# Two head masks moved from GpSimd to VectorE at the start of a convolution-and-MLP kernel

## Chip, cores, metric

One core of a Trainium2 chip. The metric is the device time of one execution in microseconds. A profile's span is some 1.8 us shorter than the time of the same run. All positions below are microseconds from the start of the profile's span.

## The reference

```python
# x [8, 4096, 192], weight [8 heads, 7 taps], w_in [192, 2048], w_out [2048, 192]
w = softmax(weight, axis=-1)
x_pad = concatenate([zeros((B, 6, D)), x], axis=1)       # causal, 7 taps
a = einsum('hk,bskhg->bshg', w, x_unf)                   # one filter per head of 24 channels
h = a.reshape(32768, 192) @ w_in
g = where(h > 0, h, exp(minimum(h, 0)) - 1)
out = g @ w_out
```

## The kernel before

The kernel works through 32 tiles of 1024 tokens. For each, TensorE convolves with a banded weight matrix `Tm`, multiplies by `w_in` into PSUM (`H`), ScalarE takes the exponential into `E`, GpSimd clips it, VectorE combines it with `H` into `gT`, and TensorE multiplies by `w_out`. The kernel gives each engine its own list of instructions and joins the lists by semaphores. The first tile goes another way, so that TensorE starts early: x is loaded as it is (`xs`), cast (`xb`), transposed on TensorE (`xT`) and convolved with diagonal weights (`taps`). The diagonal needs each partition's own head weights. They come from one small matmul with a head mask `owner`, and the band comes from another with the weights spread by a block mask `block8`. GpSimd makes both masks before it issues any DMA:

```python
# GpSimd
g.memset(ones[:], 1.0).then_inc(s_id)
W(s_id, 1)
g.affine_select(out=ident[:], in_=ones[:], ...).then_inc(s_id)
for step in range(2):                                  # owner: two selects
    W(s_id, 2 + step)
    g.affine_select(out=owner[:, :], in_=owner[:, :] if step else ones[0:HEADS, :], ...).then_inc(s_id)
W(s_id, 4)
g.affine_select(out=block8[:, :, :], ...).then_inc(s_id)
load_w_in(0); load_w_in(1); load_w_out(0)              # 7 DMA issues
for gr in range(2): load_x(1, gr)                      # 2
load_w_out(1); load_w_out(2)                           # 2
for gr in range(2): load_x(2, gr)                      # 2
for i, (n, u) in enumerate(units):
    for to_load in x_before.get(i, ()): load_x(*to_load)   # one more at i = 0
    W(s_exp, i + 1)
    g.tensor_scalar(out=E[:, i % NE, :], ..., op0=ALU.min, op1=ALU.max).then_inc(s_clp)

# VectorE
v.memset(zw[:], 0.0); v.memset(wband[:], 0.0); v.memset(xbh[...], 0.0)
W(s_wb, 1); W(s_wq, 16)
v.tensor_reduce(wmx[:], wq[:], AXIS.X, ALU.max)        # softmax of the weights begins
# ... [cut]
W(s_id, 5); W(s_set, 5)
v.tensor_tensor(wnb[:], block8[:], wn[:, :].unsqueeze(1).to_broadcast(...), ALU.mult)

# TensorE, matmul with owner
W(s_id, 4); W(s_set, 6)
```

Of the kernel before, what the change touches and what calls it, by code (L numbers as in the profile page):

```python
# [5 lines left out]
ALU = mybir.AluOpType  # L6
# [7 lines left out]
HP = 64  # L14
FC = 128
D = 192
HEADS = 8
KSIZE = 7
# [53 lines left out]
def bass_lightweight_conv__then__act_elu_kernel(  # L72
# [46 lines left out]
    gt_at, turned, att_at, conv_begun, step = {}, {}, {0: 0.0}, {}, [0]  # L119
# [226 lines left out]
    for second in range(2):  # L346
        for rt in range(2):
            g = rt ^ second
            k, b = divmod(NP - O_AT[g], NB)
# [64 lines left out]
    with ExitStack() as stack:  # L414
        def sbuf(name, shape, dt):
            return stack.enter_context(nc.sbuf_tensor(name, shape, dt))
# [4 lines left out]
        def sema(name):  # L421
            return stack.enter_context(nc.semaphore(name))
# [3 lines left out]
        ident = sbuf("ident", [P, P], BF16)  # L426
        ones = sbuf("ones", [P, P], BF16)
# [25 lines left out]
        owner = sbuf("owner", [HEADS, P], BF16)  # L453
        block8 = sbuf("block8", [HEADS, HEADS, KSIZE], BF16)
# [11 lines left out]
        s_scr = sema("s_scr")  # L466
        s_x = [[sema(f"s_x{i}_{g}") for g in range(2)] for i in range(NXB)]
        s_id = sema("s_id")
        s_xs = sema("s_xs")
        s_xh = sema("s_xh")  # L470
        s_wb = sema("s_wb")
# [143 lines left out]
        @block.gpsimd  # L615
        def _gpsimd(g: bass.BassGpSimd):
            W = Waits(g)

            def load_x(s, gr):
                b = s % NXB  # L620
                if s >= NXB:
                    W(s_cv, CU * (s - NXB))
                if s == NXB:
                    W(s_zw, 1)
                def windows(w0, w1, rows):
                    src = bass.AP(
                        tensor=x_flat.tensor,
                        offset=(s * SUP + gr * GS + w0 * CW - PAD) * D,
                        ap=[[D, rows], [CW * D, w1 - w0], [1, D]],
                    )  # L630
                    g.dma_start(  # L631
                        xg[0:rows, b, 2 * w0 + gr : 2 * w1 : 2, :], src
                    ).then_inc(s_x[b][gr], 16)

                if s == NS - 1 and gr == 1:
                    windows(0, NWIN - 1, P)
                elif gr == 2:
                    W(s_xl, 16)
                    g.tensor_copy(xg[0:XL, b, 2 * NWIN - 1, :], xl[:, :]).then_inc(s_xc)
                else:  # L640
                    windows(0, NWIN, P)

            def batch_zeros(s):

                W(s_x[s % NXB][0], x_need[s, 0])
                g.memset(xg[0:PAD, s % NXB, 0, :], 0.0).then_inc(s_z)

            def load_w_in(k):
                c0, c1 = WCOLS[k]
                for j in range(3):  # L650
                    g.dma_start(  # L651
                        w_in[0:HP, j, c0:c1],
                        bass.AP(
                            tensor=moe_w_in.tensor,
                            offset=8 * j * FF + c0,
                            ap=[[CPH * FF, HEADS], [FF, 8], [1, c1 - c0]],
                        ),
                    ).then_inc(s_w[k], 16)

            def load_w_out(k):  # L660
                q = slice(WOUT[k], WOUT[k + 1])
                g.dma_start(  # L662
                    w_out[:, q, :], moe_w_out.rearrange("(q p) d -> p q d", p=FC)[:, q, :]
                ).then_inc(s_w[3 + k], 16)

            g.memset(ones[:], 1.0).then_inc(s_id)  # L666
            W(s_id, 1)
            g.affine_select(  # L668
                out=ident[:],
                in_=ones[:],  # L670
                pattern=[[-1, P]],
                compare_op=ALU.is_equal,
                fill=0.0,
                base=0,
                channel_multiplier=1,
            ).then_inc(s_id)
            for step in range(2):
                W(s_id, 2 + step)
                g.affine_select(  # L679
                    out=owner[:, :],  # L680
                    in_=owner[:, :] if step else ones[0:HEADS, :],
                    pattern=[[0, 2], [1 - 2 * step, HP]],
                    compare_op=ALU.is_ge,
                    fill=0.0,
                    base=7 * step,
                    channel_multiplier=8 * (2 * step - 1),
                ).then_inc(s_id)
            W(s_id, 4)
            g.affine_select(  # L689
                out=block8[:, :, :],  # L690
                in_=ones[0:HEADS, 0 : HEADS * KSIZE].rearrange("p (h k) -> p h k", h=HEADS),
                pattern=[[1, HEADS], [0, KSIZE]],
                compare_op=ALU.is_equal,
                fill=0.0,
                base=0,
                channel_multiplier=-1,
            ).then_inc(s_id)
            load_w_in(0)
            load_w_in(1)
            load_w_out(0)  # L700
            for gr in range(2):
                load_x(1, gr)
            load_w_out(1)
            load_w_out(2)
            for gr in range(2):
                load_x(2, gr)
            for i, (n, u) in enumerate(units):
                s, at_n = divmod(i // 2, NQ)
                if i % 2 == 0 and at_n == ZERO_AT and (s + 2) % SPB == 0 and s + 2 < NS:
                    batch_zeros(s + 2)  # L710
                for to_load in x_before.get(i, ()):
                    load_x(*to_load)
                W(s_exp, i + 1)
                g.tensor_scalar(  # L714
                    out=E[:, i % NE, :],
                    in0=E[:, i % NE, :],
                    scalar1=1.0,
                    scalar2=0.0,
                    op0=ALU.min,
                    op1=ALU.max,  # L720
                ).then_inc(s_clp)
# [50 lines left out]
        def _vector(v):  # L772
            W = Waits(v)

            v.memset(zw[:], 0.0).then_inc(s_zw)  # L775
            v.memset(wband[:], 0.0).then_inc(s_wb)
            v.memset(xbh[:, :, :, :], 0.0).then_inc(s_xz)
            W(s_wb, 1)
            W(s_wq, 16)
            v.tensor_reduce(wmx[:], wq[:], AXIS.X, ALU.max).then_inc(s_set)  # L780
# [2 lines left out]
                out=wq2[:],  # L783
# [11 lines left out]
                out=wn[:],  # L795
# [2 lines left out]
                scalar2=None,  # L798
                op0=ALU.mult,
            ).then_inc(s_set)  # L800
            W(s_id, 5)
            W(s_set, 5)
            v.tensor_tensor(
                wnb[:],
# [32 lines left out]
            for i in range(ON_DVE):  # L837
# [3 lines left out]
                if i == 0:  # L841
                    ins = v.tensor_scalar(
                        out=part[:], in0=src, scalar1=w, scalar2=None, op0=ALU.mult
                    )
                else:
                    W(s_part, i)
                    ins = v.scalar_tensor_tensor(
                        out=part[:], in0=src, scalar=w, in1=part[:], op0=ALU.mult, op1=ALU.add
# [11 lines left out]
            for item in dve_order:  # L860
# [6 lines left out]
                if s >= NG3:  # L867
# [4 lines left out]
                    out=gT[:, s % NG3, q, u, :],  # L872
# [8 lines left out]
        def _tensor(pe):  # L881
            W = Waits(pe)
# [18 lines left out]
            for item in pe_order:  # L901
# [6 lines left out]
                    for _ in range(item[2]):  # L908
                        pe.matmul(H[:, bank, :], zw[:, 0:P], zw[:, 0:GS], start=True, stop=True)  # L909
                elif item[0] == "s":  # L910
                    W(s_id, 4)
                    W(s_set, 6)
                    pe.matmul(
                        H[:, bank_of["d", 2], 0:KSIZE],
# [73 lines left out]
                elif item[0] == "c":  # L988
# [13 lines left out]
                    h = HU * u + q  # L1002
# [36 lines left out]
                else:  # L1039
                    _, k, g, rt, q, kb, visit, ends = item  # L1040
# [93 lines left out]
```

## Time and profile before

| | before |
|---|---|
| median of the 3 runs given first | 718.48 us (718.13 to 719.18) |
| profile span | 716.6 us |
| TensorE busy | 710.7 us |
| x (`xs`) lands | 5.41 |
| first hidden-layer matmul | 10.55 |
| first clip on GpSimd | 12.86 |
| `Tm` lands, first convolution matmul | 18.70, 19.14 |

A line of a timeline gives the start, the length, the engine, the source line, the operation with what it writes and reads, how often it ran in a row, and in brackets the idle time before it with what ended it. Two lines of GpSimd's timeline of the kernel before:

```profile
2.43 3.56 POOL L651 DMA_DIRECT2D w_in<-in_moe_w_in_dram  x6
...
12.86 8.10 POOL L714 TENSOR_SCALAR E<-E 128x512 f32<-128x512 f32 x14
```

There is no bracket at the first clip: GpSimd came to it straight from a DMA issue, so it was GpSimd that was late. The intent of the change follows from this.

### The profile page before, as it was taken

How to read it: one execution, taken by the hardware profiler on the slowest of the kernel's cores; microseconds unless marked ns; L12 is line 12 of the kernel's file. 1: busy time of each engine (PE TensorE's matmuls, PEld its weight loads, DVE VectorE, ACT ScalarE, POOL GpSimd, SP SyncE). 2: the span in 40 equal slices, each digit the busy share in tenths (PEclk: the TensorE clock that was granted, in tenths of full speed). 3: DMA queues.
4: the chain of work that ended last, by engine and by line, in shares of the span. 5: the costliest groups of instructions: out<-in, count | busy, mean ns of one | idle time of the engine just before them, and what ended most of it. 6: DMA issues, size and time to landing. Idle time of an engine off the chain costs nothing.

```text
span 716.6 us, 27662 instructions
## 1 busy us (share of the span) xinstructions
PE 710.7 (99%) x11873; PEld 681.6 (95%) x11873; DVE 641.5 (90%) x1049; ACT 677.4 (95%) x1290; POOL 663.6 (93%) x1112
## 2 busy tenths in 40 slices
PE   8999999999999999999999999999999999999998
PEld 4699999999999999999999999999999999999998
DVE  7999889998898998899998999988989988999994
ACT  6999999999999999999999999999999999999994
POOL 9999999999999999999999999999999999999893
PEclk9999999999999999999999999999999999999999
DMA  9635334564433544444554344544445534444212
GB/s 183 99 72 95 65 73 78 93 86 76 80 79 74 95 89 64 80 85 79 87 91 69 73 76 95 87 73 76 85 73 91 93 63 78 87 80 83 63 43 69
DMA packets 132303, 58.80 MB, mean 82 GB/s; under 512 B 98374, under 2 KB 131412, under 8 KB 132180
## 3 DMA queue, kind: packets, MB, share of 16 engines
q0 software_dynamic: 43504, 16.77, 22.4%
q1 hardware_dynamic: 88388, 39.37, 22.0%
q8 instruction: 93, 1.52, 0.9%
q10 hardware_dynamic: 288, 0.88, 0.4%
q14 instruction: 30, 0.25, 0.1%
HBM read 34.63 MB, written 25.46 MB: 84 GB/s over the span
## 4 chain that ended last, share of the span: by engine, by line
PE 96%; POOL 2%; ACT 1%; DVE 0%; issue 0%; DVEq 0%; POOLq 0%
PE H L1052 54%; PE H L1029 37%; PE H L1004 4%; POOL xg L631 1%; ACT E L760 1%; POOL E L714 1%; POOL w_in L651 0%; POOL w_out L662 0%; DVE gT L871 0%; ACT csb L756 0%; POOL owner L679 0%; DVE osb L862 0%; POOL block L689 0%; POOL ident L668 0%; POOL ones L666 0%
## 5 line engine op out<-in xcount | busy, mean ns | idle before, releaser
L871 DVE SCALAR_TENSOR_TENSOR gT<-E,H 128x512 f16<-128x512 f32 x1024 | 631.8, 681 | 62.8 <-POOL E L714 58.4
L1029 PE MATMUL H<-att,w_in 64*128 64x512 bf16 x3072 | 679.8, 376 | 1.2 <-DVE gT L871 0.9
L1052 PE MATMUL H<-w_out,gT 64*128 64x192 f16 x8192 | 680.4, 243 | 0.1
L714 POOL TENSOR_SCALAR E<-E 128x512 f32<-128x512 f32 x1024 | 603.0, 611 | 41.1 <-ACT E L760 34.2
L1052 PEld LDWEIGHTS H<-w_out,gT 64*128 64x128 f16 x8192 | 606.7, 94 | 17.5 <-PE H L1052 1.5
L760 ACT ACTIVATE E<-H 128x512 f32<-128x512 f32 x1024 | 585.0, 601 | 23.9 <-PE H L1029 0.4
L1029 PEld LDWEIGHTS H<-att,w_in 64*128 64x128 bf16 x3072 | 275.3, 93 | 7.8 <-DVE gT L871 2.9
L1004 PE MATMUL H<-xg,Tm 64*128 64x240 bf16 x496 | 90.9, 263 | 0.0
L756 ACT ACTIVATE csb<-H 112x480 bf16<-112x480 f32 x124 | 70.7, 570 | 0.4 <-PE H L1004 0.3
L767 ACT ACTIVATE osb<-H 128x384 f32<-128x384 f32 (+1 forms) x129 | 62.0, 482 | 6.9 <-PE H L1052 6.8
L631 POOL DMA_DIRECT2D xg<-in_x_dram x62 | 54.7, 884 | 0.2 <-issue 0.2
L1004 PEld LDWEIGHTS H<-xg,Tm 64*128 64x128 bf16 x496 | 42.6, 94 | 1.2 <-DVE gT L871 0.3
L862 DVE COPY osb<-H 128x192 f32<-128x192 f32 x1 | 0.4, 357 | 7.3 <-PE H L1052 7.3
L909 PE MATMUL H<-zw 128*128 128x512 bf16 x10 | 4.3, 588 | 1.2 <-DVE zw L775 1.2
L909 PEld LDWEIGHTS H<-zw 128*128 128x128 bf16 x10 | 1.2, 134 | 3.0 <-issue 1.7
L651 POOL DMA_DIRECT2D w_in<-in_moe_w_in_dram x6 | 3.6, 612 | 0.0
L736 ACT ACTIVATE xb<-xs 128x512 bf16<-128x512 f32 x2 | 1.2, 622 | 2.4 <-DMA xs<-in_x_dram 2.4
L978 PE MATMUL H<-xT,taps 64*64 64x256 bf16 (+1 forms) x50 | 2.6, 317 | 0.0
L662 POOL DMA_DIRECT2D w_out<-in_moe_w_out_dram x3 | 2.5, 853 | 0.0
L978 PEld LDWEIGHTS H<-xT,taps 64*64 64x64 bf16 x50 | 2.0, 106 | 0.5 <-issue 0.2
L729 ACT ACT_TABLE_LOAD x1 | 1.3, 1283 | 1.2 <-PEq L1119 1.2
L936 PEld LDWEIGHTS H<-ident,xb 64*64 64x64 bf16 x48 | 1.2, 126 | 0.8 <-ACT xb L736 0.8
(45 smaller groups left out, 20.5 us busy)
## 6 DMA issues: line engine op xcount, KB each, us to landing
out_dram<-osb SPq DMA_DIRECT2D x126, 192.0 KB, 2.9
xg<-in_x_dram POOLq DMA_DIRECT2D x61, 240.0 KB, 4.5
xs<-in_x_dram ACTq DMA_DIRECT2D x1, 768.0 KB, 4.6
w_in<-in_moe_w_in_dram POOLq DMA_DIRECT2D x6, 128.0 KB, 4.7
att<-csb SPq DMA_TRANSPOSE x31, 3.9
w_out<-in_moe_w_out_dram POOLq DMA_DIRECT2D x2, 192.0 KB, 7.9
w_out<-in_moe_w_out_dram POOLq DMA_DIRECT2D x1, 384.0 KB, 11.8
w_in<-w_in SPq DMA_DIRECT2D x1, 336.0 KB, 6.8
```

What stands on the lines that cost most here:

```text
L631: g.dma_start(xg[0:rows, b, 2 * w0 + gr : 2 * w1 : 2, :], src).then_inc(s_x[b][gr], 16)
L651: g.dma_start(w_in[0:HP, j, c0:c1], bass.AP(tensor=moe_w_in.tensor, offset=8 * j * FF + c0, ap=[[CPH * FF, HEADS], [FF, 8], [1, c1 - c0]], ...
L714: g.tensor_scalar(out=E[:, i % NE, :], in0=E[:, i % NE, :], scalar1=1.0, scalar2=0.0, op0=ALU.min, op1=ALU.max,).then_inc(s_clp)
L756: a.activation(*conv_evac(W, m), ACT.Copy).then_inc(s_ce)
L760: a.activation(E[:, i % NE, :], H[:, bank_of[item], :], ACT.Exp).then_inc(s_exp)
L767: a.activation(*out_evac(W, *item[1:]), ACT.Copy).then_inc(s_oev[item[2]])
L871: v.scalar_tensor_tensor(out=gT[:, s % NG3, q, u, :], in0=E[:, i % NE, :], scalar=1.0, in1=H[:, bank_of[item], :], op0=ALU.subtract, op1=A ...
L909: pe.matmul(H[:, bank, :], zw[:, 0:P], zw[:, 0:GS], start=True, stop=True)
L978: ins = pe.matmul(H[to, bank_of["d", j] + (j == 2 and c0 > 0), c0:c1], taps[rows, tap, rows], xT[rows, j, HALO - PAD + tap + c0 : HALO - P ...
L1004: ins = pe.matmul(H[:, bank_of["c", m], 256 * q : 256 * q + UC], Tm[rows, h, :], xg[rows, s % NXB, :, CPH * h : CPH * (h + 1)].rearrange(" ...
L1029: ins = pe.matmul(H[:, bank_of[item[:3]], :], w_in[HP * r : HP * (r + 1), j, FC * q : FC * (q + 1)], att[HP * r : HP * (r + 1), s % 2, j, ...
L1052: ins = pe.matmul(acc_of(k, g)[:, D * kb : D * (kb + 1)], gT[HP * rt : HP * (rt + 1), t % NG3, q, g, t0 : t0 + P], w_out[HP * rt : HP * (r ...
```

## The change

The masks are copies of parts of the identity, so VectorE, which waits for the weights' DMA anyway (0.26 us in the profile before), can write both from it. GpSimd then issues `w_in` right after the identity.

```diff
+        s_own = sema("s_own")
 ...
-            for step in range(2):
-                W(s_id, 2 + step)
-                g.affine_select(out=owner[:, :], ...).then_inc(s_id)
-            W(s_id, 4)
-            g.affine_select(out=block8[:, :, :], ...).then_inc(s_id)
             load_w_in(0)
 ...  (VectorE, after the three memsets)
+            W(s_id, 2)
+            v.tensor_copy(owner[...],  ident[0:8, 0:8] broadcast to [8, 2, 8, 8]).then_inc(s_own)
+            v.tensor_copy(block8[...], ident[0:8, 0:8] broadcast to [8, 8, 7]).then_inc(s_own)
 ...
-            W(s_id, 5)
+            W(s_own, 2)
             W(s_set, 5)
 ...  (TensorE)
-                    W(s_id, 4)
+                    W(s_id, 2)
                     W(s_set, 6)
```

More of the change, by code (lines that the diff above doesn't have):

```diff
@@ L676, in _gpsimd @@
             ).then_inc(s_id)
-            for step in range(2):
-                W(s_id, 2 + step)
-                g.affine_select(
-                    out=owner[:, :],
-                    in_=owner[:, :] if step else ones[0:HEADS, :],
-                    pattern=[[0, 2], [1 - 2 * step, HP]],
-                    compare_op=ALU.is_ge,
-                    fill=0.0,
-                    base=7 * step,
-                    channel_multiplier=8 * (2 * step - 1),
-                ).then_inc(s_id)
-            W(s_id, 4)
-            g.affine_select(
-                out=block8[:, :, :],
-                in_=ones[0:HEADS, 0 : HEADS * KSIZE].rearrange("p (h k) -> p h k", h=HEADS),
-                pattern=[[1, HEADS], [0, KSIZE]],
-                compare_op=ALU.is_equal,
-                fill=0.0,
-                base=0,
-                channel_multiplier=-1,
-            ).then_inc(s_id)
             load_w_in(0)
@@ L777, in _vector @@
             v.memset(xbh[:, :, :, :], 0.0).then_inc(s_xz)
+            W(s_id, 2)
+            v.tensor_copy(
+                owner[:, :].rearrange("p (g h e) -> p g h e", g=2, e=8),
+                ident[0:HEADS, 0:HEADS]
+                .unsqueeze(1)
+                .unsqueeze(3)
+                .to_broadcast([HEADS, 2, HEADS, 8]),
+            ).then_inc(s_own)
+            v.tensor_copy(
+                block8[:, :, :],
+                ident[0:HEADS, 0:HEADS].unsqueeze(2).to_broadcast([HEADS, HEADS, KSIZE]),
+            ).then_inc(s_own)
             W(s_wb, 1)
```

## The prediction

> **What bounds the kernel now.** I read four things in this order: the page's totals, the chain that ended last in order of time, the timelines of the first 30 us engine by engine, and the DMA issues with their time to landing.
>
> The totals first:
>
> ```profile
> span 716.6 us, 27662 instructions
> PE 710.7 (99%) x11873; PEld 681.6 (95%) x11873; DVE 641.5 (90%) x1049; ACT 677.4 (95%) x1290; POOL 663.6 (93%) x1112
> ```
>
> TensorE is busy for 710.7 of 716.6 us, and the change touches none of its work. So a gain can only come from TensorE's own pauses, and these lie in the start-up. The chain that ended last shows which, as start, length and what ran:
>
> ```profile
> 0.79 0.21 POOL ones L666
> 1.01 0.07 issue
> 1.07 0.30 POOL ident L668
> 1.37 0.06 issue
> 1.43 0.30 POOL owner L679
> 1.73 0.06 issue
> 1.79 0.30 POOL owner L679
> 2.09 0.06 issue
> 2.14 0.33 POOL block L689
> 2.48 0.73 POOL w_in L651
> ...
> 12.84 0.02 issue
> 12.86 0.64 POOL E L714
> 13.50 0.02 issue
> 13.52 0.70 DVE gT L871
> 14.22 0.05 issue
> 14.27 1.45 PE H L1029 x7
> ```
>
> The reader is to see that the chain of the whole program starts on GpSimd: ones, identity, three mask steps, then fourteen DMA issues without a gap up to 12.84, then the first clip of E, the first product gT, and the matmul that had waited for a free PSUM bank. That matmul started 1152 ns after the one before it, where 216 ns is the pace; this pause of 0.94 us is the largest that TensorE has after its first hidden-layer matmul (10.55). After about 27 us the chain is TensorE alone.
>
> Now what else the first clip needs, and how much room VectorE has, from the timelines of ScalarE and VectorE:
>
> ```profile
> 11.39 3.53 ACT L760 ACTIVATE E<-H 128x512 f32<-128x512 f32 x7
> ```
>
> ```profile
> 1.77 0.22 DVE L777 MEMSET xbh<- 8x192 uint32 x1
> 2.25 0.15 DVE L780 TENSOR_REDUCE wmx<-wq 8x1 f32<-8x7 f32 x1 [0.26 <-DMA wq<-in_weight_dram]
> ```
>
> The first exponential ends at 11.98, 0.88 us before the clip that reads it starts: GpSimd is late, not its input. VectorE idles 0.26 us for the weights' DMA just where the copies go in.
>
> Last, the issues that feed the second tile's convolution, and its first matmuls on TensorE:
>
> ```profile
> conv_band<-wband SPq DMA_DIRECT2D x1, 288.0 KB, 6.5
> Tm<-conv_band SPq DMA_DIRECT2D x1, 256.0 KB, 5.3
> ```
>
> ```profile
> 19.14 0.26 PE L1004 MATMUL H<-xg,Tm 64*128 64x240 bf16 x1
> ```
>
> The band is issued at 6.86 and lands at 13.37, its skewed copy Tm is issued at 13.38 and lands at 18.70, and the convolution reads it at 19.14. So there is 0.44 us of slack behind GpSimd's chain, and no more.
>
> [...] from 1.5 to 4 us the ScalarE queue with x has 83.4% of the sixteen engines and GpSimd's queue 0.5%[...]. From 5 to 10 us GpSimd's queue alone has 100.7%, and the band, issued at 6.86, moves its first packet at 10.5. [...] The trace has 0.22 us for the memset of 8x192 and 0.18 us for the 8x56 product, so I take 0.22 and 0.18.
>
> **The change part by part.** Removed from GpSimd: three affine selects and their waits. The w_in issue moves from 2.43, where the timeline starts it, to the end of the identity at 1.37 plus the usual 0.06: 1.43. That is 1.00 us, by the chain 0.36 + 0.35 + 0.33 = 1.04. The fourteen issues run back to back, so GpSimd would be free at 12.84 - 1.0 = 11.84.
>
> Added to VectorE: two copies after the third memset, which ends at 1.99. With 0.22 + 0.18 us they end at about 2.39 and the maximum over the weights starts at 2.40 instead of 2.25. Of this 0.15, the next steps absorb most: the exponential of the weights starts at 2.86 only because ScalarE's table load and its two dummies hold it (the subtraction it needs ended at 2.66), about 0.14 us of room. So the copies delay the softmax, the taps and the first attention tile by 0 to 0.1 us. I take 0.03.
>
> Gained at the first clip: it may start at the later of GpSimd's 11.84 and the first exponential's end, 11.98 + 0.08 (the usual 81 ns from ScalarE to GpSimd) + 0.03 = 12.09. That is 12.86 - 12.09 = 0.77 us. The first gT and the waiting matmul follow at fixed distances, so TensorE resumes at 13.50 instead of 14.27 and its pause shrinks from 0.94 to 0.17. From there to 19.8 GpSimd runs clip after clip at 575 ns without a gap, 0.7 to 0.77 ahead. ScalarE, which had waited 0.44 us for TensorE at 17.51 and then ran at TensorE's pace of 600 ns, catches up as well (its own pace is 487).
>
> Lost again at the convolution: TensorE would arrive there at 19.14 - 0.75 = 18.39, but Tm does not land before 18.70 if its DMAs stay where they are[...]. With 0.1 us from landing to matmul it goes at 18.8. Then 0.75 becomes 0.34. The stretch from 20.6 to 24.7 is ScalarE without a pause and only shifts, and after that TensorE carries it to the end. Sum: -1.0 at GpSimd, +0.23 for the exponential, +0.02 along the clips, +0.41 for Tm: about -0.35 us.
>
> Do the DMAs move? The engines are full from about 4.1 us on (0.9 or more of sixteen), and the x load holds them until then. So w_in issued 1 us earlier finds the engines occupied and can win at most the start-up dip between 4.0 and 4.5, perhaps 0.1 to 0.2 us. I leave the landings where they are.
>
> **The rivals.** First, the full gain: w_in wins its dip, the band and Tm land 0.4 us earlier, and 0.77 us arrives at the end: 717.7. For it: the queue is in order and starts earlier. Against: the saturated engines. Second, the gain is eaten: GpSimd's queue is now further ahead when SyncE issues the band, [...] Tm lands 0.4 to 1.3 us later. Then TensorE stands at the convolution and the time is 718.5 to 719.4. For it: both band and Tm waited 3.6 us from issue to first packet[...], and it may fall either way. Third, w_in now competes with x, whose landing at 5.41 starts the whole first tile; a delay of x shifts everything by as much, up to 0.5 us, to 718.7. Against it: no x packet was interrupted by w_in before. [...]
>
> **Range and chances.** The middle is 718.48 - 0.35 = 718.1 us. The rivals span 717.7 to 719.4, and the three runs before lie 1.05 us apart (718.13 to 719.18), which is more than the effect. I set 717.3 to 719.0. A change of 2% is 14.4 us; the change can touch 1 us of TensorE's pauses, so faster and slower get 0.01 each and the same gets 0.98.
>
> **What would show it right or wrong.** Right: no mask step on GpSimd, its first w_in issue at about 1.43, the first clip at about 12.1, the matmul after the pause at about 13.5, two VectorE copies near 2.0 to 2.4 with the maximum at about 2.4, and a new pause of TensorE before the first convolution matmul at about 18.8. Wrong in the first step: the first clip still at 12.8 (slower issues). Wrong in the second: the first exponential later than 11.5, from x landing after 5.5 or from the copies. Wrong in the third: Tm landing far from 18.7, either way. If the end moves by another amount than TensorE's pauses before 27 us, the reading that TensorE alone carries the rest is wrong.

-1.0 + 0.23 + 0.02 + 0.41 is -0.34, the "about -0.35", and the 0.22 and 0.18 us for the copies are the trace's. The second rival has no measured size: its 0.4 to 1.3 us are the author's guess, as are the first's 0.4, the third's 0.5 and the 0.1 us from `Tm`'s landing to the matmul. That TensorE stands at the convolution until `Tm` is there was an assumption too; a_again shows it below, with 0.2 us idle. Two statements were without their numbers. The queue is in order: in the profile before, the last completions of GpSimd's transfers came in the order of their issue, from 8.82 us (the first three of `w_in`) and 11.38 (the other three) to 24.84. No x packet was interrupted: the eleven x packets that start from 4 us on, when `w_in` runs as well (its first packet starts at 3.95), took 234 to 236 ns, where the median of all 128 is 234.

## The result

The changed kernel took 718.97 us (median of 6 runs, 718.33 to 719.98), the kernel before in the same rounds 718.40 us (median of 6). The ratio is the mean time of one kernel's fast runs over that of the other's of the same rounds, so not quite the ratio of these medians: 1.0008, with a 95% interval from 0.9995 to 1.0021. That is "same". The total lay in the predicted range; the 0.35 us that was to be gained is not to be seen.

The page of the changed kernel, its first lines and the engines of its chain:

```profile
span 718.1 us, 27661 instructions
PE 712.4 (99%) x11873; PEld 682.8 (95%) x11873; DVE 642.7 (90%) x1051; ACT 677.0 (94%) x1290; POOL 662.7 (92%) x1109
...
PE 97%; ACT 1%; DMA 1%; POOL 1%; DVE 0%; issue 0%; DVEq 0%
```

A DMA has come into the chain, which before had none. The chain in order of time shows which, and that GpSimd's start has left it:

```profile
0.80 5.30 DMA xs<-in_x_dram
6.10 0.02 issue
6.12 0.64 ACT xb L716
6.76 0.04 issue
6.80 1.46 PE H L928 x28
```

GpSimd's timeline after, to be read against the two lines of before:

```profile
1.45 3.56 POOL L652 DMA_DIRECT2D w_in<-in_moe_w_in_dram  x6
...
14.01 8.16 POOL L694 TENSOR_SCALAR E<-E 128x512 f32<-128x512 f32 x14 [2.29 <-ACT E L740]
```

The first issue moved from 2.43 to 1.45 as planned. But the first clip came at 14.01 instead of 12.86, and GpSimd idled 2.29 us for the exponential. The input was late now, since x landed at 6.10 instead of 5.41 and TensorE was slower. Its timelines, before and then after, warm-up matmuls and transposes:

```profile
4.38 1.53 PE L909 MATMUL H<-zw 128*128 128x512 bf16 x4
6.12 0.86 PE L936 MATMUL H<-ident,xb 64*64 64x64 bf16 x32 [0.21 <-ACT xb L736]
```

```profile
4.26 1.89 PE L901 MATMUL H<-zw 128*128 128x512 bf16 x4
6.80 1.46 PE L928 MATMUL H<-ident,xb 64*64 64x64 bf16 x32 [0.66 <-ACT xb L716]
```

The same 32 transposes took 1.46 instead of 0.86 us. The trace's record of the granted clock goes with this: full speed begins at 5.41 before and at 10.23 after (in a_third below, with x as late but full speed from 6.05, they took 0.86 us). One profile of each kernel can't tell whether this moment follows the change or varies from run to run. If it varies, this profile, of the slowest of the six runs, is a poor witness of the change. And there is a second thing in it, at the other end. From TensorE's last matmul to the end of the span it is 2.94 us before (713.67 to 716.61) and 3.29 us after (714.82 to 718.11). The DMA queues and issues of that last stretch, before and then after:

```profile
q1 hardware_dynamic: 709, 0.49, 46.3%
q10 hardware_dynamic: 144, 0.10, 9.2%
...
out_dram<-osb ACTq DMA_DIRECT2D x1, 96.0 KB, 1.7
```

```profile
q1 hardware_dynamic: 666, 0.46, 41.2%
q10 hardware_dynamic: 144, 0.10, 8.7%
q14 instruction: 1, 0.01, 0.8%
...
out_dram<-osb ACTq DMA_DIRECT2D x1, 96.0 KB, 2.3
```

After, one packet of queue 14, 8192 bytes at 716.0, falls among the last output DMAs, and ScalarE's output DMA lands 2.3 us after its issue instead of 1.7. Before, the same packet comes at 717.7, when all is over. The profile gives queue 14 the kind `instruction`, so I take its packets for refills of the engines' instructions and call them so; for which engine one comes, the trace doesn't say. VectorE's stream is two instructions longer after the change (1089 records in the trace instead of 1087).

So four theories went to the chip. **Start-up**: the prediction's own, a gain of some 0.3 us before 31 us. **Landing**: the earlier `w_in` delays the completion of x. **Clock**: the moment at which the clock opens differs from run to run whatever the kernel, and made the first profile slow. **Refill**: the two VectorE instructions move an instruction refill into the last output group and cost more than the start-up gains.

### The profile page after: what moved, and what is told of

It is laid out like the page before. It is cut to its first block, busy times and chain, and to the rows that moved or that the text cites. A ratio compares the mean times of both kernels' runs of the same rounds, so it can differ in the third digit from the quotient of the medians.

```text
span 718.1 us, 27661 instructions
## 1 busy us (share of the span) xinstructions
PE 712.4 (99%) x11873; PEld 682.8 (95%) x11873; DVE 642.7 (90%) x1051; ACT 677.0 (94%) x1290; POOL 662.7 (92%) x1109
## 4 chain that ended last, share of the span: by engine, by line
PE 97%; ACT 1%; DMA 1%; POOL 1%; DVE 0%; issue 0%; DVEq 0%
PE H L1044 54%; PE H L1021 38%; PE H L996 4%; DMA xs<-in_x_dram 1%; ACT E L740 1%; POOL E L694 0%; PE H L970 0%; PE H L928 0%; ACT csb L736 0%; DVE gT L863 0%; POOL xg L632 0%; ACT xb L716 0%; DVE osb L854 0%; PE H L939 0%; DVEq L513 0%
## 5 line engine op out<-in xcount | busy, mean ns | idle before, releaser
L740 ACT ACTIVATE E<-H 128x512 f32<-128x512 f32 x1024 | 584.7, 601 | 23.5
L928 PE MATMUL H<-ident,xb 64*64 64x64 bf16 x48 | 2.5, 340 | 0.7 <-ACT xb L716 0.7
```

What stands on the lines that cost most here:

```text
L740: a.activation(E[:, i % NE, :], H[:, bank_of[item], :], ACT.Exp).then_inc(s_exp)
L928: ins = pe.matmul(H[to, bank_of[item], i:GS:XI], xb[rows, j, i, :], ident[rows, rows], start=(i == 0), stop=(i == XI - 1), tile_position=( ...
```

## The experiments

Twelve kernels were run, four at a time, each group on one chip with the kernel before run beside it. All gave correct results. This table has what the traces show; the text below refers to it. "100th" is the start of the hundredth hidden-layer matmul, "tail" the time from TensorE's last matmul to the end of the span, "refill" the queue-14 packet nearest the end that isn't common to all.

| kernel | x lands | clock opens | first hidden matmul | first clip | first conv matmul | 100th | last matmul ends | tail | refill | median of its runs (before beside it) |
|---|---|---|---|---|---|---|---|---|---|---|
| before | 5.41 | 5.41 | 10.55 | 12.86 | 19.14 | 31.36 | 713.67 | 2.94 | 717.7 | 718.40 |
| b_again | 5.42 | 6.62 | 11.22 | 12.76 | 19.09 | 31.32 | 713.88 | 2.79 | 717.8 | 718.68 (718.85) |
| b_x3 | 5.41 | 4.74 | 10.54 | 12.08 | 18.33 | 31.13 | 713.74 | 2.74 | 717.6 | 718.64 (718.52) |
| b_pad2 | 5.36 | 4.60 | 10.61 | 12.78 | 19.26 | 31.49 | 713.83 | 3.84 | 715.1 | 719.22 (718.52) |
| b_pad16 | 5.36 | 5.52 | 10.61 | 12.78 | 19.57 | 31.80 | 714.13 | 2.97 | 689.0 | 718.83 (718.52) |
| e_shift | 5.24 | 4.08 | 10.45 | 12.95 | 19.24 | 31.47 | 714.04 | 3.32 | 715.2 | 719.46 (718.85) |
| after | 6.10 | 10.23 | 12.22 | 14.01 | 20.27 | 32.50 | 714.82 | 3.29 | 716.0 | 718.97 (718.40) |
| a_again | 5.45 | 5.75 | 10.97 | 12.51 | 18.80 | 31.04 | 713.61 | 3.70 | 714.8 | 718.76 (718.85) |
| a_third | 6.13 | 6.05 | 11.86 | 13.40 | 20.32 | 32.56 | 715.12 | 4.06 | 716.8 | 719.38 (718.75) |
| a_warm | 5.48 | 5.86 | 10.98 | 12.51 | 18.88 | 31.12 | 713.68 | 3.65 | 715.2 | 719.20 (718.85) |
| a_pad16 | 5.38 | 7.23 | 10.97 | 12.51 | 19.40 | 31.63 | 714.21 | 2.82 | 688.0 | 718.78 (718.75) |
| a_split | 5.40 | none recorded | 10.96 | 12.49 | 18.75 | 30.98 | 713.33 | 2.73 | 717.2 | 718.38 (718.52) |
| a_split2 | 5.91 | none recorded | 11.13 | 12.66 | 18.92 | 31.16 | 713.73 | 2.81 | 717.9 | 718.39 (718.75) |
| w_first | 5.44 | 12.49 | 14.70 | 16.49 | 22.75 | 34.98 | 717.82 | 3.47 | 719.0 | 723.50 (718.75) |

### Both kernels again: b_again and a_again

No edit; each kernel is run once more.

> The kernel before once more, as a null. Landing theory (GpSimd's earlier w_in delays the completion of x): x lands at 5.3 to 5.5 us again. Clock theory (the TensorE clock opens at a time that differs from run to run, whatever the kernel): the opening may lie anywhere from 5 to 11 us and the span follows it by up to 1.2 us. Time ratio 1.000.

> The changed kernel once more. Landing theory: x lands at 6.0 to 6.2 us again, 0.7 us later than before, and the first clip is at 13 us or later. Clock theory: x lands anywhere, the clock opens earlier than the 10.2 us of the first profile and the first clip comes at 12.1 to 12.9 us. Time ratio 0.9995 to 1.0015, so the total tells little; the trace decides.

Measured: ratios 0.9998 (0.9985 to 1.0010) and 1.0002 (0.9988 to 1.0015). In a_again x landed at 5.45 and the clock opened at 5.75, so the first profile's two slow things were not the change's constant companions. With them gone, the start-up gain is there: the hundredth hidden matmul at 31.04 instead of 31.36 and 31.32, and the last one ends 0.27 us ahead of b_again's (713.61 against 713.88). Yet the span is 0.64 us longer (717.31 against 716.67), and all of the loss is in the tail: 3.70 against 2.79 us. Last stretch of a_again:

```profile
q1 hardware_dynamic: 581, 0.40, 32.0%
q10 hardware_dynamic: 144, 0.10, 7.8%
q14 instruction: 1, 0.01, 1.3%
...
out_dram<-osb ACTq DMA_DIRECT2D x1, 96.0 KB, 2.7
```

Its last output DMA has sixteen completions. Fifteen packets that signal them start by 715.52, the sixteenth at 716.38: one part of the transfer was 0.86 us behind the others, and the refill, one packet of 769 ns from 714.81, ran just before. (The trace doesn't say on which DMA engine a packet ran.) It is so in all seven profiles with a refill here: the last completion packet starts 0.37 to 1.04 us after the fourteenth, and in the other seven all sixteen start within 0.3 us.

GpSimd and TensorE in a_again, first the clip, then what TensorE's convolution line waited for:

```profile
12.51 2.93 POOL L694 TENSOR_SCALAR E<-E 128x512 f32<-128x512 f32 x5 [0.78 <-ACT E L740]
```

```profile
its engine sat idle before it (us, times) until:
  DMA Tm<-conv_band: 0.2, 1
```

The clip waited 0.78 us for the exponential, and the convolution then waited 0.2 us for `Tm`, which landed at 18.76.

### GpSimd held back, copies kept: e_shift

```diff
+            for step in range(3):
+                W(s_id, 2 + step)
+                g.affine_select(out=spare[:, :], in_=ones[0:HEADS, :], ...).then_inc(s_id)
             load_w_in(0)
```

> The changed kernel with three affine selects on a spare tile left on GpSimd, so that the two copies stay on VectorE and w_in is issued at 2.43 us as before. Landing theory: x lands at 5.3 to 5.5 us and the first clip is at 12.8 to 12.9 us as before. Rival (the copies on VectorE are what costs): x and the first attention tile stay late, the first exponential after 11.6 us. Time ratio 1.000.

Measured: ratio 1.0012 (0.9999 to 1.0024); first clip 12.95, first exponential at 11.29, x at 5.24. So the copies didn't delay the exponential. The first `w_in` issue came at 2.52, not at 2.43, which is about what the clip lost against 12.86. But the kernel's median was above that of before beside it, 719.46 against 718.85, with the refill at 715.2 and a tail of 3.32 us. The interval just reaches the expected ratio of 1.000; the trace tells more: with nearly GpSimd's old timing and only VectorE's two instructions left of the change, the long tail is still there.

### More warm-up matmuls: a_warm

```diff
-WARM = (6, 1, 4)
+WARM = (6, 1, 6)
```

Ahead of the transposes TensorE idled 0.66 us in the first profile after and 0.21 before, with full speed from 10.23 and 5.41. That the pause has to do with it was a guess from these two profiles, to be tested here.

> The changed kernel with six instead of four warm-up matmuls before the transposes, so that TensorE doesn't pause while x is late. Clock theory in the form that the pause keeps the clock closed: it opens by 8 us and the 48 transposes and 50 convolution matmuls run at full pace, first clip some 1 us earlier than 14.0. If the opening is only a matter of luck it can lie at 10 us again. Landing theory: x still lands at 6.0 to 6.2 us. Time ratio 0.999 to 1.000.

Measured: ratio 1.0003 (0.9991 to 1.0016). The clock opened at 5.86, but so it did in a_again without the extra matmuls, and x landed at 5.48, so there was no pause to fill: the extra matmuls even held the transposes back, to 6.43 from 6.15. The run says nothing on the pause; it is inconclusive for the clock theory. It does repeat the gain at the start (31.12) and the loss at the end (3.65).

### VectorE instructions alone: b_pad2 and b_pad16

The kernel before, with two or sixteen memsets of 8x8 elements near 12 us, where VectorE idles (1.68 us up to 13.52 in the profile before).

```diff
+            for i in range(2):            # 16 in b_pad16
+                v.memset(spare[:, i, :], 0.0)
```

> The kernel before with two tiny memsets added to VectorE's stream near 12 us, where VectorE idles. Refill theory (the two added VectorE instructions bring the refill of an instruction stream, one 8192-byte packet of queue 14, from after the end into the last output group): the packet shows at 714 to 716 us instead of 717.7, the last output DMA lands 2.3 to 2.7 us after its issue instead of 1.7 to 1.8, the span is 0.5 to 0.9 us longer, ratio 1.0007 to 1.0012. Rival (the tail is longer only where GpSimd's stream or start-up changed): tail as before, ratio 1.000.

> The kernel before with sixteen tiny memsets at the same place. Refill theory: the refill comes some 14 VectorE instructions, about 9 us, earlier than with two, at 703 to 707 us, where it meets no last output group: the last output DMA lands in 1.7 to 1.8 us again and the ratio is 0.9995 to 1.0005, although more was added than with two. Rival (each added VectorE instruction costs time): ratio above that of two memsets.

Measured: two memsets 719.22 against 718.52 us, ratio 1.0008 (0.9995 to 1.0020), tail 3.84; sixteen 718.83, ratio 1.0002 (0.9989 to 1.0014), tail 2.97. The last stretch with two, then with sixteen:

```profile
q1 hardware_dynamic: 709, 0.49, 38.6%
q10 hardware_dynamic: 144, 0.10, 7.6%
q14 instruction: 1, 0.01, 1.0%
...
out_dram<-osb SPq DMA_DIRECT2D x3, 96.0 KB, 1.9
out_dram<-osb ACTq DMA_DIRECT2D x1, 96.0 KB, 1.8
```

```profile
q1 hardware_dynamic: 703, 0.49, 47.4%
q10 hardware_dynamic: 144, 0.10, 9.5%
...
out_dram<-osb ACTq DMA_DIRECT2D x1, 96.0 KB, 2.0
```

Neither ratio is clear of noise, but the five times with two memsets (719.03 to 719.41) lie above eight of the nine beside them (718.40 to 718.72, and one of 719.67). Nothing of the change is in these kernels but a count of instructions. Two put the refill at 715.1 and made the tail 0.9 to 1.0 us longer; fourteen more moved it to 689.0 and the tail was back. Here the late transfer was one of SyncE's (it landed at 717.20), not ScalarE's as expected; it was SyncE's in a_third too, and ScalarE's in the five others with a refill at the end. The refill came at 689.0, not at 703 to 707 as I had counted, so my count of instructions per refill was off.

Sixteen weren't free either: the convolution began at 19.57 instead of 19.14. A refill goes with it again. Queue 14 and `Tm` in the stretch from 12.5 to 20 us of b_pad16:

```profile
q14 instruction: 1, 0.01, 0.3%
...
Tm<-conv_band SPq DMA_DIRECT2D x1, 256.0 KB, 6.5
```

An early refill, at 23.5 with two memsets, came at 17.7, in the middle of `Tm`'s packets. Fifteen of `Tm`'s sixteen completions arrived by 18.30, the last at 19.52.

### The gain without the instructions: a_split and a_split2

VectorE multiplies by the identity in place of the block mask, and ScalarE copies the head mask while it waits for x. VectorE has 1087 records again.

```diff
+            W(s_id, 2)                       # ScalarE, after wex
+            a.activation(owner[...], ident[0:8, 0:8] broadcast to [8, 2, 8, 8], ACT.Copy).then_inc(s_own)
 ...  (VectorE)
-            W(s_id, 2)
-            v.tensor_copy(owner[...], ...)
-            v.tensor_copy(block8[...], ...)
-            W(s_own, 2)
+            W(s_id, 2)
             W(s_set, 5)
-            v.tensor_tensor(wnb[:], block8[:], ...)
+            v.tensor_tensor(wnb[:], ident[0:8, 0:8] broadcast to [8, 8, 7], ...)
 ...  (TensorE)
-                    W(s_id, 2)
+                    W(s_own, 1)
```

> GpSimd leaves after the identity as in the changed kernel, but VectorE has no copies: the product reads the identity itself in place of the block mask, and ScalarE copies the head mask while it waits for x. VectorE has as many instructions as before. Refill theory: no queue-14 packet between 713 and 717 us, last output DMA in 1.7 to 1.9 us, and the 0.3 us of the start-up reach the end: ratio 0.9993 to 0.9998, span 716.2 to 716.5. ScalarE's one more instruction could move a refill of its own. Landing theory (early w_in delays x): x lands at 6 us or later; rival, that was one draw: 5.2 to 5.6 us.

> The version without copies on VectorE once more. Refill theory: no refill between 713 and 717 us, 2.7 to 2.9 us from the last matmul to the end, span 716.0 to 716.4 unless the slow start-up (x late, clock late) is drawn, ratio 0.9993 to 1.0003.

Last stretch of a_split:

```profile
q1 hardware_dynamic: 591, 0.40, 43.5%
q10 hardware_dynamic: 144, 0.10, 10.6%
...
out_dram<-osb ACTq DMA_DIRECT2D x1, 96.0 KB, 1.7
```

No refill, tails of 2.73 and 2.81 us, and the first profile has the shortest span, 716.06. The medians are 718.38 and 718.39 us, beside 718.52 and 718.75 of the kernel before. The ratios, however, are 1.0001 (0.9989 to 1.0014) and 1.0002 (0.9989 to 1.0014): six of the ten runs took 717.95 to 718.39, and four took 719.66 to 719.91. The measured ratio of a_split misses the expected 0.9993 to 0.9998, though its interval covers them. A version that beats both kernels is not shown. What the slow four are is taken up below.

### Time for GpSimd by another way: b_x3

```diff
-X3_AT = (0, 48)
+X3_AT = (14, 48)
```

> The kernel before, its masks on GpSimd, with one of the fourteen early DMA issues moved from ahead of the first clip to ahead of the fifteenth, which frees GpSimd 0.87 us earlier without an earlier w_in. The prediction's reading of the start-up: first clip at 12.1 us or wherever the first exponential allows, a wait for Tm at the convolution near 18.8, the 100th hidden matmul 0.2 to 0.35 us earlier than before, unless the later issue costs it again at 21 to 23 us; tail as before, ratio 0.9994 to 1.0002.

GpSimd's timeline in b_x3:

```profile
12.08 8.15 POOL L714 TENSOR_SCALAR E<-E 128x512 f32<-128x512 f32 x14
20.18 0.90 POOL L631 DMA_DIRECT2D xg<-in_x_dram  x1
```

Measured: ratio 1.0005 (0.9991 to 1.0018), above the expected 0.9994 to 1.0002, which lies within its interval. The first clip moved by 0.78 us to 12.08, and the convolution to 18.33, right behind `Tm`, which landed at 18.25 here and not near 18.8 as expected. At the hundredth hidden matmul 0.2 us of this was left (31.13), and the last matmul ended where it does before. The postponed issue stands between two clips at 20.18, as feared. It shows that the first clip is GpSimd's own fault up to 12.08, and that what is gained there is capped at `Tm`.

### Padding the changed kernel, and an exaggeration: a_pad16, a_third, w_first

a_pad16 is the changed kernel with the sixteen memsets; a_third is unedited; w_first has

```diff
+            load_w_in(0)
+            load_w_in(1)
             g.memset(ones[:], 1.0).then_inc(s_id)
 ...
-            load_w_in(0)
-            load_w_in(1)
```

> The changed kernel with sixteen tiny memsets more on VectorE, near 12 us. Refill theory: the refill moves from the last output group to about 689 us, the stretch from TensorE's last matmul to the end shrinks from 3.3 to 3.7 us to 2.7 to 3.0, and the kernel with more instructions is faster than the changed one: span 716.5 to 717.0, ratio 0.9995 to 1.0002. Rival (the longer end comes with the change's start-up in some other way): 3.3 to 3.7 us again, ratio 1.0005 or more.

> The changed kernel a third time. The reading so far: 100th hidden matmul at 31.0 to 31.1 us (0.3 earlier than before) unless the slow start-up is drawn, refill at 714 to 716 us, 3.3 to 3.7 us from last matmul to end, ratio 1.0002 to 1.001. Landing theory: x at 6 us or later; rival: 5.2 to 5.6.

> An exaggeration: the changed kernel with the six w_in issues ahead of ones and identity, so that w_in is issued 0.6 us earlier still, at 0.8 us, and its packets are ready when x starts. Landing theory (early w_in delays x): x lands at 6.5 us or later in this profile. Rival ([...] the 6.1 us was one draw): x lands at 5.2 to 5.6 us. The identity comes 3.5 us later here and delays softmax and transposes, so the time is worse under both: ratio 1.001 to 1.004.

a_pad16: ratio 1.0002 (0.9988 to 1.0016), span 717.03, tail 2.82. More instructions brought the short tail back in the changed kernel too, but its start lost the gain, with `Tm` landing at 19.35 as in b_pad16 (a refill at 16.8). a_third: ratio 1.0009 (0.9997 to 1.0022), x at 6.13: the slow start-up was drawn. Its refill, at 716.8, and its tail of 4.06 us lie past what was expected. w_first: ratio 1.0065 (1.0051 to 1.0079), so the identity's delay cost more than the expected 1.001 to 1.004. Its point was x, which landed at 5.44. But the exaggeration failed: the issue moved only from 1.45 to 1.31, not to 0.8, so it is one more draw rather than a stronger dose.

### What stays open: the slow start-up

x landed at 5.9 to 6.1 in three of the eight profiles with an early `w_in` and at 5.2 to 5.4 in all six with `w_in` at the old time. Its data are hardly late. The last x packet ended at 5.01 in the first profile after, at 4.88 in a_split2 and at 5.23 in a_third, and at 5.04 before. The early `w_in` moved its first packet no earlier, at 4.05 in the first profile after and at 3.95 before. The queues from 1.5 to 4 us, in the changed kernel:

```profile
q10 hardware_dynamic: 117, 0.72, 80.8%
q1 hardware_dynamic: 16, 0.00, 0.3%
```

No packet of GpSimd's queue is in it, though `w_in` had been issued from 1.45 on. What came late were the last three of x's sixteen completions: in the first profile after at 5.50, 5.77 and 6.10, before at 5.15, 5.20 and 5.41. The packets that signal them (sixteen of 4 bytes in x's queue) had ended at nearly the same times, the last at 5.02 after and 5.04 before; so it is the way from this packet to the arrival that took 1.08 us instead of 0.37. And until 5.4 us GpSimd's queue had started 173, 181 and 192 packets in the three profiles with a late x, and 128 to 147 in the other eleven. Late completions thus go with a burst of `w_in` packets, as the landing theory would have it; which of the two leads was tested by no run. Among single times, counting those over 0.8 us above the median of their own kernel's rounds, there are 7 of 40 with an early `w_in` and 2 of 58 with `w_in` at the old time. I made this rule after seeing the times (with 0.7 us it would be 7 of 40 against 5 of 58), and a_split2's profile with x at 5.91 was itself among the quick runs, so this is a suspicion and not a finding.

## Why the prediction was right or wrong

**The range and the verdict** came true: 718.97 in 717.3 to 719.0, and "same". There is luck in this. The median lies 0.03 us below the end of the range and 0.9 us above its middle, 718.1; the two later medians of the same kernel were 718.76 and 719.38, the second outside. And "same" leaves 14.4 us to either side.

**GpSimd 1.0 us earlier**: right. Its first `w_in` issue is at 1.44 to 1.45 in every profile of the changed kernel, and its fourteen issues end 1.0 to 1.1 us earlier, at 11.73 in a_again against 12.84 before and 12.73 in b_again.

**The copies cost 0 to 0.1 us**: right in size. They ran from 1.92 to about 2.2, and the maximum began at 2.23 to 2.40. e_shift's first exponential is at 11.29, against 11.39 before.

**First clip at 12.09**: wrong in a_again, a_warm, a_pad16 and a_split, where it is at 12.49 to 12.51. The failing term is the first exponential, taken as 0.03 us later and measured 0.42 later (11.81). Neither of the causes that the prediction named for this was at work: x had landed by 5.48 in all four, and a_split has no copies on VectorE. In a_again one VectorE instruction carries most of it. VectorE's timelines, before and a_again:

```profile
7.61 0.49 DVE L842 TENSOR_SCALAR part<-xT,wcol 128x512 f32<-128x512 bf16 x1
```

```profile
7.64 0.88 DVE L834 TENSOR_SCALAR part<-xT,wcol 128x512 f32<-128x512 bf16 x1
```

In a_again, a_warm, a_pad16 and a_split it started at 7.64, 7.92, 8.01 and 7.68 and ended at 8.52 or 8.53 in all four, as an instruction does that is let go by something else. The traces show what it goes with: in ten of the fourteen profiles it ended 0.25 us after the end of one of GpSimd's DMA issues (8.27 in a_again), and in the other four, before among them, it took 0.49 us. So it looks as if GpSimd's issue held VectorE, for which the prediction's sum had no term. b_again, where the instruction took 0.89 us, shows that it isn't the change's alone; but with GpSimd's issues 1 us earlier, another of them stood in the way. The coincidence is in the traces; that the one holds the other was tested by no run.

**Lost again at `Tm`, 0.41 us**: the mechanism is right, the size is not. a_again waited 0.2 us there, since 0.42 us had been lost before. In b_x3, whose exponential was on time, `Tm` was the stop: landed at 18.25, read at 18.33. From landing to matmul it is 0.08 us there and 0.04 in a_again, where 0.1 was guessed. The two errors cancel.

**A gain of 0.35 us at the start**: nearly right where x was on time. It is 0.30 in a_again, 0.36 in a_split, 0.22 in a_warm and 0.18 in a_split2 (hundredth hidden matmul, against 31.34, the mean of the two profiles of before); the profiles of after and a_third, with x late, lost 1.2 us there, and in a_pad16 the refill at `Tm` took the gain. At the last matmul it is 0.05 to 0.45 (against 713.78), because the long stretch between differs from profile to profile, whatever the kernel: from the hundredth hidden matmul to the end of the last matmul it takes 682.31 to 682.35 us in five profiles and 682.56 to 682.61 in eight, both kernels in each group (w_first 682.84). Why, I don't know. Within a group the gain is kept: a_again is 0.28 us ahead of b_again at the hundredth and 0.27 at the last.

**"TensorE alone carries it to the end"**: this step failed. It is true to the last matmul, and then 2.8 us remain that no matmul carries. The sum had no term for them. The profile before already had them: of the 5.9 us in which TensorE isn't busy, which the prediction placed in the start-up, 2.94 lie after the last matmul. Over the fourteen profiles the tail is 2.73 to 2.97 us, mean 2.83, in the seven where no refill meets the last outputs, and 3.29 to 4.06, mean 3.62, in the seven where one does: 0.79 us. In the profiles of a_again and b_again the balance is -0.27 at the last matmul and +0.91 in the tail, together the +0.64 us of the spans. b_pad2 shows the tail's part alone, with nothing of the change but the count, and its five runs are 0.7 us longer by the medians. The totals follow the tail only roughly: by the medians, five of the six kernels with a refill there are 0.35 to 0.70 us above the kernel before beside them and a_again is 0.09 below (w_first, slow for another reason, left out), and the six without are 0.36 below to 0.31 above.

**The rivals**: none of them was this one. "The gain is eaten" was right as an outcome, but by `Tm`, which didn't happen: `Tm` landed at 18.76 in a_again. The third, a delay of x, was put aside because no x packet had been interrupted. None was in the first profile after either (the eleven from 4 us on took 233 to 244 ns); yet x's completion came late (6.10 instead of 5.41) without its data being late (5.01 against 5.04), and the prediction hadn't told these apart. Whether the early `w_in` does it is open.

**The clock** was not in the prediction at all. It opened from 4.1 to 10.2 us in profiles of kernels that don't differ there (10.23, 5.75 and 6.05 in the three of the changed kernel; between 4.08 and 7.23 in ten of the fourteen, and at 12.49 in w_first, whose transposes came late), and where x is late as well, as in the first profile after, the first clip comes 1.15 us later than before. a_third tells the two apart, as far as one profile can: with x as late (6.13) but the clock open at 6.05, its first clip is at 13.40, where a_again has 12.51 and after 14.01. So some 0.9 us go with x and 0.6 with the clock, and at the hundredth hidden matmul the clock's share is gone (32.56 in a_third, 32.50 in after). Between 5.75 (a_again) and 7.23 (a_pad16) the opening didn't move the first clip at all (12.51 in both).

**Small readings**: the band's first packet is at 10.57 and the two waits from issue to first packet are 3.7 us (6.86 to 10.57 for the band, 13.38 to 17.10 for `Tm`), where the prediction has 10.5 and 3.6; over the fourteen profiles they are 2.5 to 4.2 us for the band and 3.7 to 3.8 for `Tm`; ScalarE's own pace is 477 to 493 ns, where it has 487. Nothing hangs on them.

## What to carry to other kernels

When a change is worth less than a microsecond, look at the whole span, its last stretch too, and take several profiles of each kernel: here a late x (1.2 us at the hundredth hidden matmul) and a refill among the last outputs (a tail of 3.62 instead of 2.83 us in the mean) each hid it. Two memsets more on VectorE moved a refill from 717.7 to 715.1 us, and sixteen to 689.0, so a pad of idle instructions is the control that tells a change's work from its count. And before counting on an earlier DMA issue, ask which transfer the next stage waits for at the end; here it was `Tm`, on another queue, which landed at 18.76 in a_again and at 18.70 before. DMA issues at another time can also meet other instructions: here one of VectorE's then took 0.88 instead of 0.49 us.
